# New order of the first Mlp's elementwise steps, with three PSUM banks for its up product and one for its reciprocal

## The chip, the cores and the metric

One core of a Trainium2 chip. The metric is device microseconds of one execution, from start to end on that core. Engines: TensorE (PE) multiplies matrices, VectorE (DVE), ScalarE (ACT) and GpSimd (POOL) do elementwise work, SyncE (SP) issues most transfers. Each engine runs its own instructions in program order and waits on semaphores for the others.

## The reference

A delta-rule attention (4 x 8 heads, 768 steps) gives x of 3072 tokens by 384. Two Mlps follow, each 384 to 2048 to 384. The first, on which the change bears, is

```
h = x @ w_in
P = a0 + a1 h + a2 h^2 + a3 h^3
Q = 1 + |b0| |h| + |b1| h^2
out = (P / (Q + 1e-6)) @ w_out
```

The second has h tanh(softplus(h)) in place of P / Q.

## The kernel before

The attention fills the first 317 us. Then come the Mlps as a loop over **units**: unit i is one of 6 groups of 512 tokens with one of 16 slices of 128 hidden columns, so units 0 to 95 are the first Mlp's and 96 to 191 the second's. Units 0 to 2 are done inside the attention; the loop begins with unit 3. A unit of the first Mlp is nine matmuls up into a PSUM bank `h` (128 x 512; nine, since both operands are split in a high and a low part), a chain of elementwise steps that ends in `gh` (high and low part of g = P / Q), and nine matmuls down that add `gh` times `w_out` into three banks `o`.

`MLP_OPS` writes out the order of one pass of the loop by hand, one string for each Mlp. `u` is the up product, `d` the down product, `y` the evacuation of a finished group's `o` banks (`ev`), `x..` the split of the next group's x into `x_hi` (ScalarE, `xa`) and `x_lo` (VectorE, `xB`), `f c` pieces of the conversion of the second Mlp's weights. `LAGS` says how many passes behind the up product a step runs. The steps of unit i, with the lines of the profile:

- `1a` ScalarE, |h| into q (L929); `1b` b1 q + b0 into r, on GpSimd for odd units and near a group's end (L932), else on ScalarE (L936); `1c` ScalarE, a3 h + a2 into s (L938); `1d` GpSimd, product q r (L942). Lag 0.
- `1e`, `1f` ScalarE, Ln and Exp: the reciprocal, into a PSUM bank `r` (L950, L952). Lag 1.
- `1g`, `1h` VectorE, s times h, then (s + a1) h (L957, L959): the last readers of `h`. Lag 0.
- `1i`, `1j`, `1k` VectorE, one Newton step and P times the reciprocal, with `r` as operand (L966, L970, L975). Lag 1.
- `1L` ScalarE and `1m` GpSimd, the high and the low part of `gh` (L909, L913). Lag 2. The down product has lag 4.

The conversion's VectorE pieces are L749 with L753, L759 and L765; its ScalarE pieces L744 and L772, its GpSimd piece L777. `Ring` hands out tiles of a tag in turn; a tile waits until the last reader of the tile that had its place is done. The eight PSUM banks are two `h`, four `o`, two `r`.

Of the kernel before, what the change touches and what calls it, by code (L numbers as in the profile page):

```python
# [33 lines left out]


MLP_OPS = [
    "fx fw y0 y1 1e 1f u0 u1 u2 1a 1b 1c 1i 1j 1k 1d 1g 1h y2 d0 d1 d2 d3 xa 1L 1m xB f c",
    "fx fw y0 1e 1f y1 2a 2b u0 u1 u2 1i 1j 1k y2 d0 v0 2M d1 v1 d2 v2 d3 v3 xa 1L 1m xB f c",
]
LAGS = {  # L40
# [6 lines left out]
class Ring:  # L47
# [6 lines left out]
    def add(self, pool, **bufs):  # L54
        for tag, b in bufs.items():
            slots = self.slots.setdefault(tag, [])
            self.n[tag] = len(slots)
            slots.extend((pool, b) for _ in range(b))

    def tile(self, shape, dtype, tag):  # L60
        i = self.n[tag]
        self.n[tag] = (i + 1) % len(self.slots[tag])
        pool, b = self.slots[tag][i]
        return pool.tile(shape, dtype, tag=tag, name=tag, bufs=b)


# [174 lines left out]
class Attention:  # L241
# [68 lines left out]
    def load(self, tile, src, u, two=False):  # L310
        o = tile.rearrange("p (n c) d -> p c n d", c=2)
        for a in range(2):
            for c in range(2):
                (self.nc.scalar if two and a else self.nc.sync).dma_start(
                    out=o[64 * a:64 * a + 64, c, :, 0:self.D], in_=src[a][a ^ c][C * u:C * u + C]
                )

    def load_v(self, tile, u):
        o = tile.rearrange("p (c n) d -> p c n d", c=2)
        for a in range(2):  # L320
            for c in range(2):
                self.nc.sync.dma_start(out=o[64 * a:64 * a + 64, c], in_=self.vv[a][c][C * u:C * u + C])
# [594 lines left out]
class Mlp1(Mlp):  # L917
    pool = ()
# [96 lines left out]
class Mlp2(Mlp):  # L1015


    pool = ()
# [32 lines left out]
def tile_delta_attention_two_mlps(  # L1051
# [29 lines left out]
    ps = Ring()  # L1081
# [9 lines left out]
    n1 = len(units)  # L1091
# [6 lines left out]
    def run(fns):  # L1098
        for fn in fns:
            fn()  # L1100
# [6 lines left out]
    def mlp(i):  # L1107
        return m1 if i < n1 else m2

    def starts(i):  # L1110
        return i == 0 or i == n1 or units[i][0] != units[i - 1][0]

    def down(i):

        g, f = units[i]
        m = mlp(i)
        last = i + 1 == n2 or starts(i + 1)

        def out_(d):
            def fn():  # L1120
                acc = m.acc[g][d]
                ev = sb.tile([128, TOK], F32, "ev")
                if i >= n1:
                    nc.scalar.copy(out=ev[:, 0:DM], in_=acc[:, 0:DM])
                    r0 = d * S + g * GU * C
                    nc.sync.dma_start(out=out[r0:r0 + GU * C, :], in_=ev[:, 0:DM])
                    return
                nc.scalar.copy(out=ev, in_=acc)  # L1128
                nc.sync.dma_start(out=x2[g][d * 128:(d + 1) * 128], in_=ev)
            return fn  # L1130

        fns = m.down(i, g, f, starts(i), last)
        return fns, [out_(d) for d in range(len(fns) // 3)] if last else []

    with ExitStack() as actx:
# [35 lines left out]
        for i in range(FIRST):  # L1171
# [6 lines left out]
            else:  # L1178
                r = at.kq[i - 2].rearrange("p s n t -> p (s n t)").rearrange("p (j a t) -> p j a t", j=2, a=2)
# [10 lines left out]
    with ExitStack() as bctx:  # L1190
        sb2 = bctx.enter_context(tc.tile_pool(name="sb2", bufs=1, reuse_waits="tile"))
        ps2 = bctx.enter_context(tc.tile_pool(name="ps2", bufs=1, space=PSUM, reuse_waits="tile"))
        sb.add(sb2, w=NF - FQ - FG, wt=1, w64=1, wm=1, x=1, q=3, s=3, r=2, g=3, gh=5 - FIRST, ev=3)
        ps.add(ps2, h=2, o=4, r=2)
        own = FQ + FG
        fetch_w = {n: (w1.fetch_split, own + LOOK + n) for n in range(NF - own - LOOK)}
        for f in range(DIRECT):
            fetch_w[n1 - NF + 6 + f] = (w2.fetch_split, f)
        calm = [i for i in range(CONV_START, n1 - 8) if not any(starts(i + 5 - k) for k in range(3))]
        for f in range(LOOK):  # L1200
            w1.fetch_split(own + f)
        steps = [
            (m1, "1a", m1.e1, [0]), (m1, "1b", m1.e1, [1]), (m1, "1c", m1.e1, [2]), (m1, "1d", m1.e2, None),
            (m1, "1e", m1.e3, [0]), (m1, "1f", m1.e3, [1]), (m1, "1g", m1.e4, [0]), (m1, "1h", m1.e4, [1]),
            (m1, "1i", m1.e5, [0]), (m1, "1j", m1.e5, [1]), (m1, "1k", m1.e5, [2]),
            (m1, "1l", m1.hi, "V"), (m1, "1L", m1.hi, "A"), (m1, "1P", m1.hi, "P"),
            (m1, "1m", m1.lo, "P"), (m1, "1M", m1.lo, "V"),
            (m2, "2a", m2.e1, None), (m2, "2b", m2.e2, None), (m2, "2M", m2.lo, None),
        ]
        steps = {name: (m, f, a) for m, name, f, a in steps}  # L1210
        ups, downs = {}, {}
        m1.pool = {i for i in range(n1) if i % 2 or any(starts(j) for j in range(i + 3, i + 6) if j < n2)}
        m2.pool = range(n1, n1 + NF)
        for i in range(n2 + max(LG.values())):
            kind = int(i >= n1)
            if i == CONV_START - 3:
                conv.start()

            def at_x(f):
                for k in range(3):  # L1220
                    j = i + 5 - k
                    if 0 < j < n2 and starts(j):
                        f(mlp(j))(units[j][0], k)

            for op in LISTS[kind]:
                if op in steps:
                    m, f, a = steps[op]
                    j = i - LG[op[0] + {"L": "l", "P": "l", "M": "m"}.get(op[1], op[1])]
                    if FIRST <= j < n2 and mlp(j) is m:
                        f(j, *([a] if a else []))  # L1230
                elif op[0] == "u" and FIRST <= i < n2:
                    if i not in ups:
                        ups[i] = mlp(i).up(i, *units[i])
                    n = int(op[1])
                    run(ups[i][3 * n:3 * n + 3])
                elif op[0] == "d" and 0 <= i - FIRST < FIRST:
                    if i - FIRST not in downs:
                        downs[i - FIRST] = down(i - FIRST)
                    n = int(op[1])
                    run(downs[i - FIRST][0][3 * n:3 * n + 3])  # L1240
                elif op[0] in "dvy" and FIRST <= i - LAG - (op[0] == "y") < n2:
                    j = i - LAG - (op[0] == "y")
                    if j not in downs:
                        downs[j] = down(j)
                    n = int(op[1])
                    if op[0] == "d":
                        run(downs[j][0][3 * n:3 * n + 3])
                    elif (op[0] == "y") == (j < n1):
                        run(downs[j][1][n:n + 1])
                elif op == "fw" and i in fetch_w:  # L1250
                    fetch, f = fetch_w[i]
                    fetch(f)
                elif op == "fx" and i + 8 < n2 and starts(i + 8):
                    mlp(i + 8).fetch_x(units[i + 8][0])
                elif op == "xa":
                    at_x(lambda m: m.x_hi)
                elif op == "xB":
                    at_x(lambda m: lambda g, k: m.x_lo(g, k, "V"))
                elif op == "c" and i > n1:
                    w2.free = True  # L1260
                    w2.word = w2.word or ps.tile([128, TOK], F32, "r")[:, 0:384]
                    conv.pull(CONV_RATE)
                elif op == "c" and i in calm:
                    conv.pull(6 * DIRECT * (calm.index(i) + 1) // len(calm) - conv.n)
                elif op == "f":
                    conv.flush()
# [29 lines left out]
```

## Time and profile before

| | us |
|---|---|
| median of 3 runs (lowest, highest) | 1118.54 (1116.56, 1120.43) |
| the profiled execution | 1121.15 |
| its span in the profile | 1119.4 |
| PE busy | 1074.0 (96%) |
| DVE busy | 721.4 (64%) |
| ACT busy | 611.1 (55%) |
| POOL busy | 543.5 (49%) |
| granted TensorE clock, mean | 0.983 |

The shares are means over three stages: the attention (to 317 us), the first Mlp (to about 720 us) and the second. What the change is worth is read from the first Mlp's stretch alone. A row of the timeline is start, duration, engine, line, operation, output <- inputs and the count that is merged into it.

### The profile page before, as it was taken

To read this page: it belongs to the slowest core of one execution; us is meant where nothing else is said; L and a number is where in the kernel's file an instruction comes from. 1 tells how busy PE (TensorE), PEld (TensorE's weight loads), DVE (VectorE), ACT (ScalarE), POOL (GpSimd) and SP (SyncE) were. 2 spreads that over 40 slices of the span, in tenths; PEclk is the share of its full clock that TensorE was granted. 3 is DMA by queue.
4 is the path that set the end of the run, shared out by engine and by line. 5 is a ranking of instruction groups with operands and counts; after the bars stand their busy time and mean duration, and the time that the engine had idled before them with its cause. 6 is when DMAs were issued, how large, how long until landed. Compare 5 with 4: busy or idle time off the path is not lost.

```text
span 1119.4 us, 25084 instructions
## 1 busy us (share of the span) xinstructions
PE 1074.0 (96%) x10396; PEld 935.2 (84%) x10396; DVE 721.4 (64%) x1207; ACT 611.1 (55%) x1099; POOL 543.5 (49%) x626
## 2 busy tenths in 40 slices
PE   8888899898999999999999999999999999999998
PEld 7778888788877788788887888899999999999997
DVE  5895777985779999999999999992121212112110
ACT  4434545243668888889888888643333323323322
POOL 3286987738657777777777777762000000000000
PEclk9898998999999999999999999999999999999999
DMA  9427687324464120212203046240101001010000
GB/s 130 88 50 209 185 218 212 72 60 117 102 242 154 54 72 34 84 41 74 83 15 113 4 139 240 86 155 1 57 1 57 1 22 36 1 57 1 29 1 29
DMA packets 119889, 92.94 MB, mean 83 GB/s; under 512 B 79456, under 2 KB 104160, under 8 KB 119776
## 3 DMA queue, kind: packets, MB, share of 16 engines
q1 hardware_dynamic: 117344, 90.85, 27.9%
q8 instruction: 81, 1.33, 0.5%
q10 hardware_dynamic: 2112, 0.39, 0.2%
q0 software_dynamic: 320, 0.10, 0.1%
q14 instruction: 32, 0.26, 0.1%
HBM read 63.02 MB, written 28.31 MB: 82 GB/s over the span
## 4 chain that ended last, share of the span: by engine, by line
PE 56%; POOL 15%; ACT 8%; DVE 8%; DMA 6%; issue 5%; SPq 1%; POOLq 0%; ACTq 0%; DVEq 0%
PE h L898 23%; PE o L1040 18%; PE o L1007 6%; POOL q L942 5%; DMA kn<-in_k_dram 3%; POOL gh L913 2%; DMA w<-in_moe_w_in_dram 2%; POOL r L932 2%; ACT r L950 2%; PE c_ps L602 2%; PE y_ps L640 2%; POOL xs L531 1%; POOL tmp L525 1%; ACT r L952 1%; ACT q L929 1%
## 5 line engine op out<-in xcount | busy, mean ns | idle before, releaser
L898 PE MATMUL h<-x,w 128*128 128x512 f32 x1278 | 318.0, 393 | 2.8 <-DVE s L959 2.7
L898 PEld LDWEIGHTS h<-x,w 128*128 128x128 f32 x1278 | 236.8, 188 | 55.7 <-DVE s L959 9.2
L913 DVE TENSOR_TENSOR gh<-g,gh 128x512 fp32r<-128x512 f32 x80 | 55.4, 693 | 282.7 <-ACT g L1031 282.7
L1026 ACT ACTIVATE gh<-h 128x512 fp32r<-128x512 f32 x96 | 57.7, 601 | 230.5 <-PE h L898 230.5
L1040 PE MATMUL o<-w,gh 128*128 128x384 f32 x864 | 162.4, 336 | 0.0
L1007 PE MATMUL o<-gh,w 128*128 128x512 f32 x648 | 159.1, 389 | 0.0
L1040 PEld LDWEIGHTS o<-w,gh 128*128 128x128 f32 x864 | 153.4, 188 | 6.0
L913 POOL TENSOR_TENSOR gh<-g,gh 128x512 fp32r<-128x512 f32 x109 | 141.3, 1297 | 23.9 <-ACT g L1031 21.4
L942 POOL TENSOR_TENSOR q<-q,r 128x512 f32<-128x512 f32 x93 | 120.7, 1298 | 60.2 <-ACT r L936 55.8
L1007 PEld LDWEIGHTS o<-gh,w 128*128 128x128 f32 x648 | 121.5, 188 | 26.0 <-ACT ev L1128 0.8
L898 PE MATMUL h<-x,wg 128*128 128x512 f32 x423 | 105.0, 392 | 1.2 <-DVE s L959 1.2
L898 PEld LDWEIGHTS h<-x,wg 128*128 128x128 f32 x423 | 78.7, 188 | 18.0 <-DVE s L959 2.5
L950 ACT ACTIVATE r<-q,cst 128x512 f32<-128x512 f32 x93 | 64.3, 692 | 47.8 <-POOL q L942 47.7
L966 DVE SCALAR_TENSOR_TENSOR q<-q,r 128x512 f32<-128x512 f32 x93 | 63.2, 679 | 14.0 <-ACT r L952 13.7
L938 ACT ACTIVATE s<-h,ab 128x512 f32<-128x512 f32 x93 | 72.0, 774 | 0.0
L959 DVE SCALAR_TENSOR_TENSOR s<-s,ab,h 128x512 f32<-128x512 f32 x93 | 69.6, 748 | 3.3
L970 DVE SCALAR_TENSOR_TENSOR r<-s,ab,r 128x512 f32<-128x512 f32 x93 | 69.4, 746 | 0.0
L531 POOL TENSOR_TENSOR xs<-xs,tmp 128x30 f32<-128x30 f32 (+14 forms) x120 | 63.8, 532 | 9.4
L957 DVE TENSOR_TENSOR s<-s,h 128x512 f32<-128x512 f32 x93 | 63.3, 681 | 4.2 <-ACT s L938 4.2
L975 DVE SCALAR_TENSOR_TENSOR g<-q,r 128x512 f32<-128x512 f32 x93 | 63.9, 687 | 3.2
L525 POOL TENSOR_TENSOR tmp<-xs 128x30 f32<-128x30 f32 (+14 forms) x120 | 58.5, 487 | 7.1
L932 POOL TENSOR_SCALAR r<-q,ab 128x512 f32<-128x512 f32 x53 | 41.4, 782 | 35.3 <-ACT q L929 35.3
(183 smaller groups left out, 1755.2 us busy)
## 6 DMA issues: line engine op xcount, KB each, us to landing
w<-w SPq DMA_DIRECT2D x24, 768.0 KB, 6.7
w<-in_moe_w_in_dram SPq DMA_DIRECT2D x32, 384.0 KB, 3.8
w<-in_moe_w_out_dram SPq DMA_DIRECT2D x32, 384.0 KB, 3.7
xraw<-x SPq DMA_DIRECT2D x36, 256.0 KB, 4.1
w<-wt SPq DMA_DIRECT2D x8, 768.0 KB, 3.3
gh<-in_q_dram SPq DMA_DIRECT2D x48, 96.0 KB, 3.4
v<-in_v_dram SPq DMA_DIRECT2D x48, 96.0 KB, 3.6
x<-yst SPq DMA_DIRECT2D x24, 192.0 KB, 3.4
```

Of the source, the lines that this page charges most:

```text
L525: eng.tensor_tensor(out=tv, in0=ls[:, j, j + 1:HC].unsqueeze(1).to_broadcast([128, j, n]), in1=xs[:, 0:j, j:j + 1].to_broadcast([128, j, n ...
L531: eng.tensor_tensor(out=xs[:, 0:j, j + 1:HC], in0=xs[:, 0:j, j + 1:HC], in1=tv, op=ALU.add)
L898: self.nc.tensor.matmul(out=self.st[i]["h"], lhsT=self.w.t[f][:, a, 0, k], rhs=self.x[g][:, b, k], start=(n == 0), stop=(n == 8),)
L913: (nc.gpsimd if engine == "P" else nc.vector).tensor_tensor(out=s["gh"][:, 1], in0=s["g"], in1=s["gh"][:, 0].bitcast(F32), op=ALU.subtract)
L938: nc.scalar.activation(out=s["s"], in_=s["h"], func=ACTF.Identity, scale=k["a3"], bias=k["a2"])
L942: nc.gpsimd.tensor_tensor(out=s["q"], in0=s["q"], in1=s["r"], op=ALU.mult)
L950: nc.scalar.activation(out=s["r"], in_=s["q"], func=ACTF.Ln, bias=k["c"])
L959: nc.vector.scalar_tensor_tensor(out=s["s"], in0=s["s"], scalar=k["a1"], in1=s["h"], op0=ALU.add, op1=ALU.mult)
L970: nc.vector.scalar_tensor_tensor(out=s["r"], in0=s["s"], scalar=k["a0"], in1=s["r"], op0=ALU.add, op1=ALU.mult)
L975: nc.vector.scalar_tensor_tensor(out=s["g"], in0=s["q"], scalar=2.0, in1=s["r"], op0=ALU.subtract, op1=ALU.mult, reverse0=True)
L1007: self.nc.tensor.matmul(out=self.acc[g][d], lhsT=self.w.t[f][:, a, 1, d], rhs=self.st[i]["gh"][:, b], start=(first and n == 0), stop=(last ...
L1040: self.nc.tensor.matmul(out=self.acc[g][t][:, 0:384], lhsT=self.st[i]["gh"][:, a, t * 128:(t + 1) * 128], rhs=self.w.t[f][:, b, 1].rearran ...
```

## The change

The first string of `MLP_OPS` gets another order: `1e 1f` move from ahead of the up product to behind `1h`, `1i 1j 1k` from ahead of `1d 1g 1h` to behind them, and `1c` goes ahead of `1b`. `Ring.lend` lets a tag take a place from another: one bank, with a tag of its own `hr`, goes to `h` in the first Mlp, and to `r` when the second begins. So the first Mlp has three banks `h`, one `r`, four `o`; the second has what it had.

```
-    "fx fw y0 y1 1e 1f u0 u1 u2 1a 1b 1c 1i 1j 1k 1d 1g 1h y2 d0 d1 d2 d3 xa 1L 1m xB f c",
+    "fx fw y0 y1 u0 u1 u2 1a 1c 1b 1d 1g 1h 1e 1f 1i 1j 1k y2 d0 d1 d2 d3 xa 1L 1m xB f c",
...
-            slots.extend((pool, b) for _ in range(b))
+            slots.extend((pool, b, tag) for _ in range(b))
+
+    def lend(self, pool, tag, to, back=None):
+        if back:
+            self.slots[back].pop()
+            self.n[back] %= len(self.slots[back])
+        self.n[to] = len(self.slots[to])
+        self.slots[to].append((pool, 1, tag))
...
-        pool, b = self.slots[tag][i]
+        pool, b, tag = self.slots[tag][i]
...
-        ps.add(ps2, h=2, o=4, r=2)
+        ps.add(ps2, h=2, o=4, r=1)
+        ps.lend(ps2, "hr", "h")
...
+            if i == n1:
+                ps.lend(ps2, "hr", "r", "h")
```

The lines of the changed kernel stand 7 higher from `Ring` on (L957 becomes L964) and 8 to 10 higher in the loop.

On VectorE, in the first group behind the attention, where one conversion piece and one `x_lo` fall (tile numbers name the allocation: `h_5320`, `h_5361` are the banks of two neighbouring units). Before:

```order
L957 TENSOR_TENSOR s_5332<-s_5332,h_5320 128x512
L959 SCALAR_TENSOR_TENSOR s_5332<-s_5332,ab_77,h_5320 128x512
L765 SCALAR_TENSOR_TENSOR wm_5230<-w64_5049,wm_5230 128x384
L966 SCALAR_TENSOR_TENSOR q_5330<-q_5330,r_5358 128x512
L970 SCALAR_TENSOR_TENSOR r_5358<-s_5332,ab_77,r_5358 128x512
L975 SCALAR_TENSOR_TENSOR g_5379<-q_5330,r_5358 128x512
L957 TENSOR_TENSOR s_5373<-s_5373,h_5361 128x512
L959 SCALAR_TENSOR_TENSOR s_5373<-s_5373,ab_77,h_5361 128x512
L882 TENSOR_TENSOR x_5393<-xraw_5234,x_5393 128x512
```

The same two passes of the changed kernel, where these two units have the banks `h_5317` and `h_5358`:

```order
L973 SCALAR_TENSOR_TENSOR q_5289<-q_5289,r_5336 128x512
L977 SCALAR_TENSOR_TENSOR r_5336<-s_5291,ab_77,r_5336 128x512
L982 SCALAR_TENSOR_TENSOR g_5341<-q_5289,r_5336 128x512
L772 SCALAR_TENSOR_TENSOR wm_5230<-w64_5049,wm_5230 128x384
L964 TENSOR_TENSOR s_5370<-s_5370,h_5358 128x512
L966 SCALAR_TENSOR_TENSOR s_5370<-s_5370,ab_77,h_5358 128x512
L973 SCALAR_TENSOR_TENSOR q_5327<-q_5327,r_5377 128x512
L977 SCALAR_TENSOR_TENSOR r_5377<-s_5329,ab_77,r_5377 128x512
L982 SCALAR_TENSOR_TENSOR g_5382<-q_5327,r_5377 128x512
L889 TENSOR_TENSOR x_5393<-xraw_5234,x_5393 128x512
```

The two steps on a new `h` (L957, L959; now L964, L966) stand ahead of the three steps on the reciprocal of the unit before, and the conversion piece and `x_lo`, which stood behind `1h`, now stand behind `1k`.

On ScalarE at the same place, before:

```order
L950 ACTIVATE r_5317<-q_5292,cst_78 128x512
L952 ACTIVATE r_5317<-r_5317 128x512
L929 ACTIVATE q_5330<-h_5320 128x512
L936 ACTIVATE r_5331<-q_5330,ab_77 128x512
L938 ACTIVATE s_5332<-h_5320,ab_77 128x512
L909 CAST gh_5352<-g_5300 128x512
```

and in the changed kernel:

```order
L936 ACTIVATE q_5327<-h_5317 128x512
L945 ACTIVATE s_5329<-h_5317,ab_77 128x512
L943 ACTIVATE r_5328<-q_5327,ab_77 128x512
L957 ACTIVATE r_5336<-q_5289,cst_78 128x512
L959 ACTIVATE r_5336<-r_5336 128x512
L916 CAST gh_5352<-g_5303 128x512
```

The steps on the new `h` now come ahead of Ln and Exp of the unit before, and `1c` ahead of `1b`. The orders of TensorE, GpSimd and SP are the same in both but for the names of the tiles.

Counted over the 89 passes from the fifth on in that listing, VectorE has no conversion piece and no `x_lo` between `1k` and the next `1g` in 23; in 18 it has an `x_lo`, in 16 each L749 with L753, L759 and L765. Of the 48 conversion places 25 follow a pass with `1b` on ScalarE (9 the pair, 8 L759, 8 L765) and 23 a pass with `1b` on GpSimd (7, 8, 8); all 18 `x_lo` follow the latter. Behind a pass that has none of these stand 8 of the 25, 9 of the 23 and 3 of the 18; behind a pass that has the pair stand 4, 5 and 2.

## Rows read from the trace of the kernel before

**Rows 1.** Windows: length, busy us (count) of PE, PEld, DVE, ACT, POOL, clock, DMA.

```profile
345.00:720.00 375.00, 371.63 (x1617) 300.87 (x1616) 357.85 (x534) 322.48 (x549) 286.69 (x247) 1.00 0.21 75
```

**Rows 2.** Timeline of TensorE, four groups of the first Mlp.

```profile
344.64 2.33 PE L898 MATMUL h<-x,w 128*128 128x512 f32 x9 [0.62 <-DVE s L959]
...
590.24 2.20 PE L1007 MATMUL o<-gh,w 128*128 128x512 f32 x9
592.28 2.20 PE L898 MATMUL h<-x,wg 128*128 128x512 f32 x9
...
712.73 2.20 PE L898 MATMUL h<-x,wg 128*128 128x512 f32 x9
```

**Rows 3.** Line 898's and VectorE's waits, 345 to 720 us: us in total, times.

```profile
  DVE s L959: 14.6, 32
...
DVE q L966 <- ACT r L952: 9.9, 17, 1.0
```

**Rows 4.** VectorE's extras by line and form, 345 to 720 us.

```profile
L882 DVE TENSOR_TENSOR x<-xraw,x 128x512 fp32r<-128x512 f32 x18 | 16.3, 906 | 0.0
L765 DVE SCALAR_TENSOR_TENSOR wm<-w,wm 128x384 int32<-128x384 int32 x16 | 15.0, 938 | 0.0
L759 DVE SCALAR_TENSOR_TENSOR wm<-w,wm 128x384 int32<-128x384 int32 x16 | 12.2, 760 | 0.0
L753 DVE TENSOR_SCALAR wm<-wm 128x384 int32<-128x384 int32 x15 | 11.0, 732 | 0.5
L749 DVE TENSOR_SCALAR wm<-wm 128x384 f32<-128x384 f32 x15 | 9.9, 658 | 0.0
```

**Rows 5.** Timeline of VectorE over one unit with an extra.

```profile
544.45 0.68 DVE L957 TENSOR_TENSOR s<-s,h 128x512 f32<-128x512 f32 x1
545.17 0.75 DVE L959 SCALAR_TENSOR_TENSOR s<-s,ab,h 128x512 f32<-128x512 f32 x1
545.83 0.78 DVE L765 SCALAR_TENSOR_TENSOR wm<-w,wm 128x384 int32<-128x384 int32 x1
546.54 0.68 DVE L966 SCALAR_TENSOR_TENSOR q<-q,r 128x512 f32<-128x512 f32 x1
547.13 0.74 DVE L970 SCALAR_TENSOR_TENSOR r<-s,ab,r 128x512 f32<-128x512 f32 x1
547.91 0.69 DVE L975 SCALAR_TENSOR_TENSOR g<-q,r 128x512 f32<-128x512 f32 x1
548.52 0.68 DVE L957 TENSOR_TENSOR s<-s,h 128x512 f32<-128x512 f32 x1
```

**Rows 6.** Timeline of ScalarE with its neighbours on GpSimd and VectorE, one unit.

```profile
474.30 0.69 ACT L950 ACTIVATE r<-q,cst 128x512 f32<-128x512 f32 x1 [1.08 <-POOL q L942]
...
475.03 0.58 ACT L952 ACTIVATE r<-r 128x512 f32<-128x512 f32 x1
475.52 0.59 ACT L929 ACTIVATE q<-h 128x512 f32<-128x512 f32 x1
475.53 0.55 DVE L759 SCALAR_TENSOR_TENSOR wm<-w,wm 128x384 int32<-128x384 int32 x1
...
476.15 0.82 ACT L936 ACTIVATE r<-q,ab 128x512 f32<-128x512 f32 x1
...
476.87 0.77 ACT L938 ACTIVATE s<-h,ab 128x512 f32<-128x512 f32 x1
477.04 1.30 POOL L942 TENSOR_TENSOR q<-q,r 128x512 f32<-128x512 f32 x1 [1.53 <-ACT r L936]
...
477.53 0.61 ACT L909 CAST gh<-g 128x512 fp32r<-128x512 f32 x1
```

**Rows 7.** GpSimd's linear step `1b` by line, 345 to 720 us.

```profile
L932 POOL TENSOR_SCALAR r<-q,ab 128x512 f32<-128x512 f32 x50 | 39.1, 782 | 30.5 <-ACT q L929 30.5
```

**Rows 8.** Timeline of GpSimd and VectorE at one `x_lo`.

```profile
361.07 1.29 POOL L913 TENSOR_TENSOR gh<-g,gh 128x512 fp32r<-128x512 f32 x1
...
361.38 1.52 DVE L882 TENSOR_TENSOR x<-xraw,x 128x512 fp32r<-128x512 f32 x1
```

## Prediction

> **What bounds the kernel now.** I read the busy table by stretches first, because the whole-page shares mix stages. In the stretch of the first Mlp (345 to 720 us) the clock is granted in full, TensorE is busy 99% and VectorE 95% [rows 1]: two engines that are both almost full. The second Mlp (from 720 us) keeps TensorE busy without a gap and the change touches only its first `r` tile, so its time is taken as it is.
>
> Next the timeline of TensorE. A group of nine matmuls follows the one before in 2.04 us [rows 2], so a unit (nine up, nine down) costs 4.08 us where nothing waits. From unit 10's first matmul at 344.64 to unit 98's at 712.73 [rows 2] lie 88 units: 368.09 us against 88 x 4.08 = 359.0. TensorE loses 9.1 us here. The view of line 898 says to whom: each wait is for step `1h` on VectorE (L959), 32 times [rows 3]. With two `h` banks, unit i+2 can't start before VectorE has done `1h` of unit i, and in the old order `1h` stands behind `1i 1j 1k` of unit i-1 and behind ScalarE's `1e 1f`.
>
> Then VectorE itself. The gaps between starts [rows 5] are 0.72 (`1g` to `1h`), 0.66 (`1h` to the next), 0.59 (`1i` to `1j`), 0.78 (`1j` to `1k`) and 0.61 (`1k` to the next): 3.36 us a unit. On top come what I call extras: one of the three `x_lo` (L882) or a piece of the weight conversion (the pair L749 and L753, or L759, or L765). By the order listing, the 89 cycles from unit 4 on hold 18 `x_lo` and 16 of each piece. With the means of [rows 4], less 0.07 because the next starts that much before an end [rows 5]: 16 x (1.39 + 0.76 + 0.94 - 0.21) + 18 x (0.906 - 0.07) = 61.1 us. VectorE therefore needs 89 x 3.36 + 61.1 = 360.1 us where TensorE needs 89 x 4.08 = 363.1. They are within 1%, so any microsecond added to VectorE soon is one added to the kernel.
>
> **The change, part by part.** *Third `h` bank, and `1g 1h` ahead of `1i 1j 1k`.* An `h` is now free as soon as ScalarE has done `1a 1c` and VectorE `1g 1h`; unit i+3 waits for it, not unit i+2. That takes away the place at which all 32 waits stand. If VectorE's work stays what it is, the most that comes back is the 9.1 us.
>
> *One bank for the reciprocal.* `1e` of unit i (Ln, into the bank) now waits for `1k` of unit i-1. Count from the start of `1k`: it runs 0.69 [rows 5], the handover is put at 0.07 as from ScalarE's L936 to GpSimd's L942 [rows 6], so `1e` starts at 0.76; `1f` 0.73 later at 1.49 and 0.58 long [rows 6], so `1i` can start at 2.14. Without the bank VectorE would be there at 0.61 + 0.72 + 0.66 = 1.99. Idle 0.15 in a cycle with no extra (23 of 89), hidden under the extra in the 66 others, since each of these takes 0.48 or more. Sum 3.5 us. In the old order VectorE's idle time of 9.9 us stands at the same step [rows 3], from the chain over GpSimd; in the new order GpSimd's product (`1d`) has a whole cycle more, so that chain no longer decides. Behind the waiting `1e` on ScalarE stand `1f`, `1L` and the next `1a`, all with a cycle to spare.
>
> *`1c` before `1b`* lets `1g` start earlier; ScalarE runs the same instructions. A cycle of it with `1b` is 0.73 + 0.49 + 0.52 + 0.49 + 0.66 + 0.72 = 3.61 us (spacings of [rows 6], those of `1L` and `1a` put at their length less 0.09), under 4.08. Nothing, but for the five cycles that also hold two evacuations; I leave these to the range. *The bank's return* at the second Mlp restores the old layout: nothing. SP's and GpSimd's orders are unchanged, no transfer moves: nothing.
>
> *Where the extras land* is the part that decides. In the old order they stand behind `1h`, in the new one behind `1k` (the order rows above). How long an extra takes depends on GpSimd: `x_lo` at 361.38 lasted 1.52 us, to 0.54 after the end of the GpSimd subtraction that began at 361.07 [rows 8], while L759 with no GpSimd instruction beside it took 0.55 [rows 6]. I read that as: the extra waits until GpSimd's instruction ends, then runs about 0.54 (`x_lo`) or 0.54 x 384/512 = 0.41 (pieces, an estimate). Both rows show the subtraction only. I take it that the product `1d` holds an extra just as long, since it has the same operands and the same 1.30 us [rows 6]; if it held none, the sum would end at rival 1. The Trainium skill ("SBUF — State Buffer", SBUF: two separate sides) says that VectorE and GpSimd share one pair of ports under an exclusive lock for a whole instruction. By that rule the product holds an extra too, and the sum stays as worked out here; the trace before has no extra beside a product to show it.
>
> Now GpSimd in the new order, from `1k` at 0: `1f` 1.49, `1L` 1.98 to 2.59, subtraction `1m` 2.66 to 3.95; `1a` 2.50, `1c` 2.99. Where ScalarE does `1b`: 3.66 to 4.48, product `1d` 4.55 to 5.85. Where GpSimd does it (0.78 [rows 7]): 3.95 to 4.73, product 4.80 to 6.10; with an `x_hi` on ScalarE all that 0.5 later. The next cycle's extra asks 0.61 after its `1k`, so after an average cycle of 4.05 at 4.66.
> - Behind a ScalarE `1b` (9 pairs, 8 L759, 8 L765): the product has just begun, wait 1.19, then 0.41. L759 1.60 for 0.76, L765 1.60 for 0.94, the pair about 1.9 for 1.39: 9 x 0.5 + 8 x 0.84 + 8 x 0.66 = +16.5 us.
> - Behind a GpSimd `1b` (7 pairs, 8 L759, 8 L765, 18 `x_lo`): single pieces slip in ahead of the product at 0.55, 8 x -0.21 + 8 x -0.39 = -4.8; a pair's second half meets the product, 7 x 0.46 = +3.2; `x_lo` waits 0.59 for the late `1b`, 1.13 for 0.91, 18 x 0.22 = +4.0. Together +2.4.
> - Cycles aren't all average. After one without extra (3.51) the ask comes at 4.12, after one with a pair at about 5.4. By the listing 8 and 4 of the first kind, 9 and 5 pieces and 3 and 2 `x_lo` of the second stand there: -8.4 - 3.0 + 4.1 + 2.8 - 0.8 + 1.2 = -4.1.
>
> Extras +14.8 us. VectorE in the new order: 360.1 + 3.5 + 14.8 = 378.4 over the same 89 cycles. That is more than TensorE's 363.1, so VectorE sets the pace and TensorE loses 15.3 instead of 9.2 (9.1 x 89/88): **+6.1 us**. The extra buffer can't help against an engine that needs more in the mean; it only moves TensorE's wait to the next thing that is late, the `gh` halves that GpSimd's `1m` and ScalarE's `1L` hand to the down product, and the evacuations at a group's end.
>
> **Bounds.** Below: no extra is held at all. Then a piece takes 0.55 and `x_lo` 0.73 at most (0.55 x 512/384): 64 x 0.48 + 18 x 0.66 = 42.6, VectorE 299.0 + 42.6 + 3.5 = 345, TensorE is the limit and all 9.2 come back. Above: the term of 14.8 half as large again, and 4 us for the five cycles with evacuations: 6.1 + 7.4 + 4 = +17.5.
>
> **Rivals.**
> 1. *Faster: the buffer does what it promises.* If extras cost what they cost now, VectorE needs 360.1 + 3.5 = 363.6 against 363.1: about 8.5 us come back, and with a little jitter 6. For it: 32 waits with one releaser [rows 3], and a mean need of VectorE just at TensorE's. Against it: an extra beside a product is what the new order makes common. It decides where the extras' sum grows by less than about 2.5 us. Time 1118.5 - 6 = 1112.5. The Trainium skill ("Perfetto Trace Analysis", Identifying Performance Opportunities) reads gaps that repeat on the engine that should be full as a sign of too few buffers; by that the whole 9.2 would return, 1109.3.
> 2. *No change.* GpSimd itself is held up by VectorE's extras and slides out of the way, so the term is half of mine: VectorE 371, TensorE loses 7.9, -1.3 us. Time about 1117 to 1120.
> 3. *Slower, by the single reciprocal bank or by ScalarE.* Cycles with `1b` on ScalarE and two evacuations are 3.61 + 2 x 0.5 (a copy is about 0.6 long by L909's 0.61 [rows 6], less 0.09) = 4.6, with a conversion step 5.1; five of them, about 4 us, if nothing hides it: on top of mine, 1129.
>
> **How the numbers follow.** The profiled execution took 1121.15 us (span 1119.4); the sum gives 1127.2 for it. The median of the runs is 1118.54, 2.6 lower, so the same difference gives 1124.6, rounded 1125. Chances: my forecast with rival 3, 0.58; rival 2, 0.19; rival 1, 0.23. Faster or slower means by over 0.3% (3.4 us), about what a measurement of this kernel can tell. The range reaches down to rival 1 and up to +14.5 of the bound of +17.5: 1112 to 1133, with some 0.12 below and 0.08 above; the forecast's own range is 1121 to 1133.
>
> **What would show it.** Right: in the stretch of the first Mlp TensorE no longer waits in line 905 (the up product) for `1h`, but in line 1014 for `gh` or `ev`, and for more time in all than 9 us; L766, L772 and the pair's second half (L760) are longer in the mean than now, some near 1.6 us with a product of GpSimd beside them; VectorE's idle time stays small. Wrong: the means of the extras stay as in [rows 4] or fall, then rival 1 or 2 holds; or VectorE idles several microseconds more before `1i`, then the bank alone costs more than the 3.5 us.

## The result, and the profile after

The changed kernel takes 1127.87 us (median of 16 executions, 1120.21 to 1132.44); the kernel before, on the same chip, 1121.46 us (16 executions, 1116.56 to 1128.32). The ratio is 1.0055, 95% interval 1.0038 to 1.0073. That is slower by more than the 0.3% that the prediction took as its bound. A second set of runs of the changed kernel (below) gave 1.0035, 1.0003 to 1.0067. The profiled execution took 1126.96 us, against 1121.15 us for the one of before.

From the page of the changed kernel, the span and the busy time by engine:

```profile
span 1125.2 us, 25174 instructions
## 1 busy us (share of the span) xinstructions
PE 1073.0 (95%) x10396; PEld 940.1 (84%) x10396; DVE 728.8 (65%) x1207; ACT 607.2 (54%) x1099; POOL 553.6 (49%) x626
```

TensorE does the same work as before, VectorE is busy 7.4 us longer and GpSimd 10.1 us longer, though neither has more instructions (1207 and 626, as before). The same window of the first Mlp as in [rows 1] (length, busy us of PE, PEld, DVE, ACT, POOL, clock, DMA):

```profile
345.00:720.00 375.00, 364.39 (x1588) 299.71 (x1587) 361.50 (x529) 318.21 (x545) 292.29 (x245) 0.99 0.21 74
```

TensorE lost 7.2 us of busy time in it and fell from 1617 to 1588 matmuls; VectorE is busier with fewer instructions. The waits in that window (us in total, times, longest), to be held against [rows 3]:

```profile
ACT r L957 <- DVE g L982: 41.7, 49, 2.4
...
PEld o L1014 <- ACT ev L1135: 12.7, 5, 3.3
PE o L1014 <- ACT ev L1135: 10.6, 5, 2.9
...
DVE q L973 <- ACT r L959: 2.4, 6, 0.5
```

TensorE no longer waits for `1h`. It waits five times, once at each group's end, for an evacuation on ScalarE. `1e` on ScalarE (L957) now waits 49 times for VectorE's `1k` (L982), the last reader of the one reciprocal bank. The timeline of TensorE, at unit 10, around one such wait, and at unit 98:

```profile
344.01 2.20 PE L905 MATMUL h<-x,w 128*128 128x512 f32 x9
...
590.09 2.20 PE L905 MATMUL h<-x,wg 128*128 128x512 f32 x9
592.13 0.84 PE L1014 MATMUL o<-gh,w 128*128 128x512 f32 x3
595.88 1.66 PE L1014 MATMUL o<-gh,w 128*128 128x512 f32 x6 [2.91 <-ACT ev L1135]
597.38 2.21 PE L905 MATMUL hr<-x,wg 128*128 128x512 f32 x9
...
718.42 2.20 PE L905 MATMUL h<-x,wg 128*128 128x512 f32 x9
```

Between a group's ends TensorE runs without a gap. At a group's end the evacuation that frees an `o` bank is late: three matmuls go into the bank that is free, the other six wait, and the next up product starts 3.2 us later than a full rate would have it (597.38 less 590.09 is 7.29, against 4.08). From unit 10 to unit 98 lie 374.41 us: TensorE loses 15.4 of them, where before it lost 9.1. Not all of this is waiting: behind two of the five waits the granted clock falls to 1.2 GHz, the lower of its two levels, for some 3 us (mean 0.79 from 388 to 396 us, 0.57 from 526 to 530), and the nine up matmuls from 527.77 on take 3.12 us instead of 2.04. From unit 10 to 98 the clock is 0.991 in the mean, about 3.4 us of TensorE's time; before it was 1.000.

VectorE's extras by line and form, the counterpart of [rows 4] (L760 was L753, L766 was L759, L889 was L882, L772 was L765, L756 was L749):

```profile
L760 DVE TENSOR_SCALAR wm<-wm 128x384 int32<-128x384 int32 x15 | 18.2, 1210 | 0.5
L766 DVE SCALAR_TENSOR_TENSOR wm<-w,wm 128x384 int32<-128x384 int32 x16 | 14.1, 883 | 0.0
L889 DVE TENSOR_TENSOR x<-xraw,x 128x512 fp32r<-128x512 f32 x18 | 14.0, 780 | 0.0
L772 DVE SCALAR_TENSOR_TENSOR wm<-w,wm 128x384 int32<-128x384 int32 x16 | 13.1, 822 | 0.0
L756 DVE TENSOR_SCALAR wm<-wm 128x384 f32<-128x384 f32 x15 | 10.8, 720 | 0.0
```

The pair's second half went from 732 to 1210 ns and L766 from 760 to 883; `x_lo` and L772 became shorter. Why is seen in the timeline of GpSimd and VectorE, four places:

```profile
361.80 1.29 POOL L939 TENSOR_SCALAR r<-q,ab 128x512 f32<-128x512 f32 x1
...
361.82 0.71 DVE L889 TENSOR_TENSOR x<-xraw,x 128x512 fp32r<-128x512 f32 x1
...
460.51 1.29 POOL L949 TENSOR_TENSOR q<-q,r 128x512 f32<-128x512 f32 x1 [2.00 <-ACT r L943]
...
460.56 1.66 DVE L766 SCALAR_TENSOR_TENSOR wm<-w,wm 128x384 int32<-128x384 int32 x1
...
526.79 0.55 DVE L766 SCALAR_TENSOR_TENSOR wm<-w,wm 128x384 int32<-128x384 int32 x1
...
541.11 1.29 POOL L949 TENSOR_TENSOR q<-q,r 128x512 f32<-128x512 f32 x1
541.27 1.34 DVE L760 TENSOR_SCALAR wm<-wm 128x384 int32<-128x384 int32 x1
```

A piece of 0.55 us (526.79, nothing of GpSimd beside it) takes 1.66 us when it asks just after a product has begun (460.56), and the pair's second half 1.34 (541.27). The other way round, at 361.8, `x_lo` gets 0.71 and GpSimd's `1b` beside it 1.29 instead of the 0.78 of [rows 7]. Whichever is held, one of the two pays.

**A ledger of VectorE.** The experiments are compared by one account, made from the timeline of VectorE between unit 10 and unit 98. Each distance from one start to the next is booked: behind `1g 1h 1i 1j 1k` the spacing of [rows 5] as base (0.716, 0.663, 0.599, 0.782, 0.605 in the mean) and what is above it as idle; behind an extra the whole distance. A wait that follows an extra is therefore booked with the extra: 7.0 us of them in e6, 1.4 to 1.6 in the two traces of the changed kernel and in e10, at most 0.5 in the others. The window also holds 83 extras in the kernel before, in e3, e6 and e10, 84 in e2, 85 in e7b and 86 in the others; three more are about 2 us. Beside it stands the stage, from the first up product of the loop (unit 3) to unit 98, and the ratio of times.

| kernel | unit 10 to 98 | base | extras | idle | stage | ratio, 95% interval |
|---|---|---|---|---|---|---|
| before | 368.1 | 294.7 | 61.2 | 11.8 | 395.6 | 1 |
| changed | 374.4 | 295.3 | 70.2 | 8.4 | 401.9 | 1.0055 (1.0038 to 1.0073) |
| changed, again | 372.8 | 296.7 | 65.8 | 10.1 | 399.5 | 1.0035 (1.0003 to 1.0067) |
| e1: order alone | 365.3 | 296.1 | 67.7 | 1.2 | 392.0 | 0.9971 (0.9942 to 1.0001) |
| e2: banks alone | 371.0 | 295.4 | 62.5 | 12.9 | 397.7 | 1.001 (0.9981 to 1.004) |
| e4: order, two `h`, one `r` | 371.2 | 295.3 | 68.8 | 6.5 | 397.9 | 1.007 (1.0034 to 1.0107) |
| e12: e4 again | 371.7 | 296.1 | 69.1 | 6.5 | 398.3 | 0.9996 (0.9961 to 1.003) |
| e3: e4, words of the pieces in PSUM | 360.7 | 295.3 | 47.6 | 17.2 | 387.4 | 0.9926 (0.9897 to 0.9955) |
| e6: e3 in the old order | 367.4 | 294.7 | 55.5 | 16.9 | 395.8 | 0.9978 (0.995 to 1.0006) |
| e5: changed, evacuations early | 370.1 | 296.1 | 64.1 | 9.6 | 396.8 | 1.0014 (0.9985 to 1.0043) |
| e10: e3, evacuations early | 360.2 | 296.1 | 48.3 | 15.6 | 386.9 | 0.9924 (0.9886 to 0.9962) |
| e11: e1, evacuations early | 365.1 | 296.1 | 68.3 | 0.7 | 391.8 | 0.9956 (0.9929 to 0.9982) |
| e7: changed, pieces behind `1h` | 369.5 | 297.4 | 61.3 | 11.2 | 396.4 | 1.0029 (0.9998 to 1.0061) |
| e7b: e1, pieces behind `1h` | 377.8 | 296.7 | 74.9 | 5.4 | 406.2 | 1.007 (1.0041 to 1.0098) |

TensorE's own 88 units are 359.0. The stage of the kernels run twice came out 2.4 us apart (changed) and 0.4 us apart (e4); the ratio of the latter moved from 1.007 (7 executions) to 0.9996 (12), more than each interval allows. The attention ahead of the stage differs from one execution to the next (unit 3 begins at 309 to 325 us), while what follows unit 98 takes 406.6 to 406.8 us in all fourteen traces. So below a per cent the stage of a trace is the better witness, and no cause is read from less than 2.5 us of it. The kernel before has one trace only.

### The profile page after: what moved, and what is told of

The parts are those of the page before. It is cut to its first block, busy times and chain, and to the rows that moved or that the text cites. A ratio compares the mean times of both kernels' runs of the same rounds, so it can differ in the third digit from the quotient of the medians.

```text
span 1125.2 us, 25174 instructions
## 1 busy us (share of the span) xinstructions
PE 1073.0 (95%) x10396; PEld 940.1 (84%) x10396; DVE 728.8 (65%) x1207; ACT 607.2 (54%) x1099; POOL 553.6 (49%) x626
## 4 chain that ended last, share of the span: by engine, by line
PE 50%; DVE 24%; ACT 9%; DMA 7%; issue 5%; POOL 3%; SPq 2%; ACTq 0%; DVEq 0%; POOLq 0%
PE h L905 19%; PE o L1047 18%; DVE q L973 4%; DVE r L977 4%; DVE g L982 4%; PE o L1014 3%; DMA w<-in_moe_w_in_dram 2%; PE y_ps L647 2%; DMA kn<-in_k_dram 2%; ACT r L957 2%; DVE s L964 2%; PE c_ps L609 2%; ACT r L959 2%; DMA w<-w 2%; SPq L321 1%
## 5 line engine op out<-in xcount | busy, mean ns | idle before, releaser
L905 PE MATMUL h<-x,w 128*128 128x512 f32 x1071 | 264.9, 391 | 0.0
L905 PEld LDWEIGHTS h<-x,w 128*128 128x128 f32 x1071 | 200.0, 188 | 38.5
L1014 PE MATMUL o<-gh,w 128*128 128x512 f32 x648 | 161.6, 393 | 10.6 <-ACT ev L1135 10.6
L1014 PEld LDWEIGHTS o<-gh,w 128*128 128x128 f32 x648 | 121.9, 189 | 38.0 <-ACT ev L1135 12.7
L949 POOL TENSOR_TENSOR q<-q,r 128x512 f32<-128x512 f32 x93 | 124.3, 1337 | 37.4 <-ACT r L943 21.7
L957 ACT ACTIVATE r<-q,cst 128x512 f32<-128x512 f32 x92 | 63.8, 694 | 45.0 <-DVE g L982 42.3
L905 PE MATMUL h<-x,wg 128*128 128x512 f32 x351 | 87.8, 395 | 0.0
L905 PEld LDWEIGHTS h<-x,wg 128*128 128x128 f32 x351 | 66.5, 190 | 13.1
L982 DVE SCALAR_TENSOR_TENSOR g<-q,r 128x512 f32<-128x512 f32 x92 | 63.2, 687 | 3.2
L916 ACT CAST gh<-g 128x512 fp32r<-128x512 f32 x93 | 57.2, 615 | 0.4 <-DVE g L982 0.4
L1038 ACT ACTIVATE g<-h 128x512 f32<-128x512 f32 x96 | 57.1, 595 | 0.0
L959 ACT ACTIVATE r<-r 128x512 f32<-128x512 f32 x92 | 53.5, 582 | 2.9
L1047 PE MATMUL o<-wg,gh 128*128 128x384 f32 x288 | 54.4, 337 | 0.0
```

The costliest lines, as they stand in the source:

```text
L905: self.nc.tensor.matmul(out=self.st[i]["h"], lhsT=self.w.t[f][:, a, 0, k], rhs=self.x[g][:, b, k], start=(n == 0), stop=(n == 8),)
L949: nc.gpsimd.tensor_tensor(out=s["q"], in0=s["q"], in1=s["r"], op=ALU.mult)
L957: nc.scalar.activation(out=s["r"], in_=s["q"], func=ACTF.Ln, bias=k["c"])
L959: nc.scalar.activation(out=s["r"], in_=s["r"], func=ACTF.Exp, scale=-1.0)
L982: nc.vector.scalar_tensor_tensor(out=s["g"], in0=s["q"], scalar=2.0, in1=s["r"], op0=ALU.subtract, op1=ALU.mult, reverse0=True)
L1014: self.nc.tensor.matmul(out=self.acc[g][d], lhsT=self.w.t[f][:, a, 1, d], rhs=self.st[i]["gh"][:, b], start=(first and n == 0), stop=(last ...
```

## The experiments

The diffs are against the changed kernel. First the change was taken apart.

**e1, the new order with the old banks** (two `h`, two `r`):

```
-        ps.add(ps2, h=2, o=4, r=1)
-        ps.lend(ps2, "hr", "h")
+        ps.add(ps2, h=2, o=4, r=2)
...
-            if i == n1:
-                ps.lend(ps2, "hr", "r", "h")
```

> New order of the steps, banks as before (two h, two r). Theory A (VectorE sets the pace, and its conversion pieces are held by GpSimd's product in the new order): the pieces last as long as in the changed kernel, 4 to 8 us slower than before; TensorE's waits go back to the up product. Rival B (the single reciprocal bank costs it): with two banks 0 to 3 us faster than before. Rival C (TensorE's waits for the evacuations cost it): with two banks TensorE can't run ahead, so no such waits and within 3 us of before.

Measured 1117.69 us, 0.9971, with an interval that just reaches 1; the stage is 3.6 us shorter than before, and 3.8 in e11, which has this order and these banks too. That is rival B's forecast and not theory A's, though the extras did grow: VectorE has almost no idle time left (1.2 us), its extras take 6.5 us more (about 2 of it for three more of them in the window), and TensorE waits for `1h` again, but less (waits of e1, first Mlp):

```profile
PEld h L905 <- DVE s L966: 7.2, 10, 1.5
PE h L905 <- DVE s L966: 3.7, 6, 1.0
...
DVE q L973 <- ACT r L959: 1.5, 3, 0.5
```

So by the stage the order alone is a gain: it takes away 10.6 us of VectorE's idle time, nearly all of it ahead of `1i`, and gives 6.5 back in extras.

**e2, the new banks with the old order:** the changed kernel with the first string of `MLP_OPS` as it was before.

> Old order, banks as in the change (three h, one r). Theory A: the pieces stand behind 1h and last as before; the third h bank gives a little back, 0 to 5 us faster than before, unless the single r bank binds. Rival B: 5 us slower or more, with VectorE idle before 1i. Rival C: TensorE runs ahead and waits for the evacuations, 4 to 8 us slower.

Measured 1121.33 us, 1.001; stage +2.1 us, within what two traces of one kernel differ. The waits of e2:

```profile
DVE q L973 <- ACT r L959: 10.1, 18, 1.0
...
PE o L1014 <- ACT ev L1135: 8.2, 5, 2.2
...
PEld h L905 <- DVE s L966: 1.8, 1, 1.8
```

The third `h` bank does take away the wait for `1h` (32 times before, once here), and TensorE then waits as long at the five evacuations. VectorE's wait for the reciprocal is what it was. Rival C named the waits, but no kernel 4 to 8 us slower came of them, and theory A's gain didn't come either.

**e4 and e12, the new order with two `h` and one `r`,** the eighth bank left empty:

```
-        ps.lend(ps2, "hr", "h")
...
-                ps.lend(ps2, "hr", "r", "h")
+                ps.lend(ps2, "hr", "r")
```

> New order, two h, one r, the eighth bank left empty in the first Mlp: the control of the run before. Theory A: as the changed kernel or up to 4 us slower than it (6 to 10 slower than before). Rival B: as the changed kernel. Rival C: within 3 us of before, as TensorE can't run ahead.

> The new order with two h banks and one for the reciprocal (the eighth bank empty), once more: the one trace of it was taken of the fastest of its executions, and its medians stood 11.7 us above those of the same order with two reciprocal banks, where the traces show only 5.9 us. Theory (the single bank costs 6 to 10 us, in idle time before 1i and in extras that meet GpSimd's product; a third h bank gives nothing back): the stage at 398 to 402 us, idle 6 to 10, extras 66 to 70, ratio 1.003 to 1.008, not to be told from the changed kernel's 1.0055. Rival (the third h bank gives or costs something by itself): the stage and the ratio more than 0.3% from the changed kernel's, to one side.

Measured 1129.41 us, 1.007, and then 1121.21 us, 0.9996. The second ratio lies below the forecast of 1.003 to 1.008. The two traces agree to half a microsecond, so they are used: stage 397.9 and 398.3, as forecast. Against e1 (392.0), which differs by the second reciprocal bank alone, the single bank costs 5.9 to 6.3 us, nearly all of it as idle time of VectorE (6.5 against 1.2). The changed kernel, which has a third `h` bank on top, is 1.2 to 4.0 us slower than these two by the traces; none shows a gain from that bank, and a cost of it is not settled. One candidate is the clock, 0.991 from unit 10 to 98 in both traces of the changed kernel and 1.000 in e4 and e12, where TensorE's longest wait for an evacuation is 1.4 us instead of 2.9; no run tests it.

**e8, the changed kernel once more,** nothing edited:

> The changed kernel once more, nothing edited: it gives the spread by which one trace may differ from another of the same kernel. If the split of VectorE's time read so far (extras 70.2, idle 8.4, 374.4 us for 88 units) is a property of the order, all three come out within 1.5 us, five waits for an evacuation included, and the stage (unit 3 to 98) within 1.5 of 401.9. If the phase of GpSimd wanders from one execution to the next, extras or idle differ by several microseconds, and readings of single terms under that size are not to be made. The ratio to before 1.003 to 1.008 either way.

Measured 1124.85 us, 1.0035. The terms moved by more than 1.5 us: extras 65.8 instead of 70.2, idle 10.1 instead of 8.4. Nearly the whole difference of the extras (4.1 of 4.4) is the pair's second half, by the lines of VectorE in e8:

```profile
L760 DVE TENSOR_SCALAR wm<-wm 128x384 int32<-128x384 int32 x15 | 14.1, 942 | 0.5
```

942 ns against 1210: the phase between VectorE and GpSimd isn't the same in each execution. So the second alternative came. What does repeat is the place of TensorE's waits (four evacuations, 8.7 us) and, to some 3 us, the sum of extras and idle time.

Then the cost under dispute, the extras that GpSimd holds.

**e3, e4 with the conversion pieces' words in the empty PSUM bank.** The same instructions, with the word that the pieces build up in PSUM instead of SBUF:

```
-        ps.add(ps2, h=2, o=4, r=1)
-        ps.lend(ps2, "hr", "h")
+        ps.add(ps2, h=2, o=4, r=1, word=1)
+        w2.word = ps.tile([128, TOK], F32, "word")[:, 0:384]
```

> New order, two h, one r, and the eighth bank as the place for the conversion pieces' intermediate words (in the second Mlp such pieces took 0.56 us beside GpSimd). Theory A: the four pieces fall to about 0.56 us each, VectorE's extras from about 70 to about 44 us, and the kernel is 5 to 9 us faster than before and at least 10 faster than the same kernel without this place. Rivals B and C: no faster than that kernel, since the bank loop and the evacuations are the same.

Measured 1113.67 us, 0.9926, faster than both kernels. This is theory A's forecast. VectorE's extras by line in e3 (the window takes in the first pieces of the second Mlp, hence more of them):

```profile
L889 DVE TENSOR_TENSOR x<-xraw,x 128x512 fp32r<-128x512 f32 x18 | 16.2, 898 | 0.0
L766 DVE SCALAR_TENSOR_TENSOR word<-w,word 128x384 int32<-128x384 int32 x21 | 11.7, 557 | 0.1
L772 DVE SCALAR_TENSOR_TENSOR wm<-w,word 128x384 int32<-128x384 int32 x21 | 11.5, 548 | 0.1
L760 DVE TENSOR_SCALAR word<-word 128x384 int32<-128x384 int32 x20 | 11.3, 566 | 0.7
L756 DVE TENSOR_SCALAR word<-wm 128x384 f32<-128x384 f32 x20 | 11.1, 554 | 0.1
```

and its timeline at one pair:

```profile
660.53 1.30 POOL L920 TENSOR_TENSOR gh<-g,gh 128x512 fp32r<-128x512 f32 x1
661.08 0.55 DVE L756 TENSOR_SCALAR word<-wm 128x384 f32<-128x384 f32 x1
661.66 0.57 DVE L760 TENSOR_SCALAR word<-word 128x384 int32<-128x384 int32 x1
```

Each piece now takes its 0.55 us, the first of these inside a GpSimd instruction and the second begun in it; only `x_lo`, left as it was, is still long (898). The extras fall from 68.8 to 47.6 us (about 2 of this is three extras fewer in the window), VectorE has 17.2 us to spare, and TensorE is within 1.7 us of its own 359.0. In the first Mlp the one thing changed against e4 is where a piece's word lies, and the stage is 10.5 us shorter: that is what the pieces held by GpSimd cost there. (In the second Mlp e3 has one reciprocal bank less; the time behind unit 98 is 406.8 us in both.)

**e6, the same words in PSUM in the old order:** e3 with the old string.

> Old order, two h, one r, the eighth bank for the conversion pieces' words. Theory A: extras fall from 61 to about 47 us as in the new order with this place, VectorE has time to spare, and the stretch comes to within 3 us of that kernel's 387.4 (4 to 8 us faster than before). If the order matters by itself (its chain of h over GpSimd to Exp holds TensorE in the old one), it stays 4 us or more behind the new order with this place.

Measured 1118.6 us, 0.9978, stage 395.8 against 395.6 before. Its waits:

```profile
DVE q L973 <- ACT r L959: 19.1, 40, 1.2
PEld h L905 <- DVE s L966: 13.1, 33, 1.8
```

The pieces do fall as forecast. With the waits behind an extra counted as idle time, the extras go from 61.0 to 48.5 us and the idle time from 12.0 to 23.9: nearly all that is saved turns into waiting for the reciprocal, and TensorE waits 33 times for `1h` as before (32). So in the old order VectorE's sum does not set the pace, and the second forecast holds (8.4 us behind e3). What does is the chain over the reciprocal, by these waits; in the new order cheaper work on VectorE pays.

Last, two places that the trace of the changed kernel pointed to.

**e5, the evacuations one pass earlier:**

```
-    "fx fw y0 y1 u0 u1 u2 1a 1c 1b 1d 1g 1h 1e 1f 1i 1j 1k y2 d0 d1 d2 d3 xa 1L 1m xB f c",
+    "fx fw u0 u1 u2 1a 1c 1b 1d 1g 1h 1e 1f 1i 1j 1k d0 d1 d2 d3 xa y0 y1 y2 1L 1m xB f c",
...
-                elif op[0] in "dvy" and FIRST <= i - LAG - (op[0] == "y") < n2:
-                    j = i - LAG - (op[0] == "y")
+                elif op[0] in "dvy" and FIRST <= i - LAG - (op[0] == "y" and kind) < n2:
+                    j = i - LAG - (op[0] == "y" and kind)
```

> The changed kernel with a group's three evacuations one pass earlier on ScalarE (behind the down product that they read, ahead of 1L). Theory A (VectorE sets the pace; the wait for the evacuations is only where TensorE's lead ends): TensorE's waits move to the gh halves or the up product, the first Mlp's stretch stays within 2 us of the changed kernel's 401.9. Rival C (the evacuations cost it): the 10.6 us of waits go and 6 to 10 us come back.

Measured 1120.53 us, 1.0014, stage 396.8: 5.1 us below the first trace of the changed kernel, 2.7 below the second. That is neither theory A's forecast (within 2) nor rival C's (6 to 10). Four waits for an evacuation are left (6.8 us), and the extras are lower too (64.1). The same edit was therefore made to two kernels in which TensorE hardly waits for an evacuation, **e10** (on e3) and **e11** (on e1).

> The pieces' words in PSUM (as in the fastest kernel so far) and the evacuations one pass earlier. Theory A (what is left there is TensorE's own time, the evacuations cost 0.8 us in one wait): the stage stays within 1.5 us of 387.4, the ratio within 0.002 of 0.9926. Rival (the evacuations take time from ScalarE and VectorE at each group's end that returns elsewhere): 2 to 4 us less, ratio about 0.990.

> The new order with the old banks (two h, two for the reciprocal) and the evacuations one pass earlier. In the order alone the trace has no wait for an evacuation that counts; VectorE is full (idle 1.2 us) and TensorE waits 7.2 us for h. Theory A (VectorE's sum decides, the waits for evacuations of the changed kernel are where its lateness shows): no gain, the stage within 2 us of 392.0 and the ratio within 0.002 of 0.9971. Rival (the place of the evacuations costs by itself, as the gain of 5 us from the same edit on the changed kernel suggests): 3 to 5 us less, ratio about 0.993.

Measured 1111.89 us, 0.9924, and 1116.52 us, 0.9956; the stages are 0.5 and 0.2 us from those of e3 and e1, as theory A has it in both. The place of the evacuations costs nothing where VectorE has time or two reciprocal banks. What the edit gave on the changed kernel is some 3 to 5 us by the traces, with intervals of the ratio that overlap; how much of that is the evacuation and how much the phase of the extras stays open.

**e7, the pieces behind `1h`,** as in the old order, with the new banks, and **e7b**, the same string with the old banks:

```
+    "fx fw y0 y1 u0 u1 u2 1a 1c 1b 1d 1g 1h c 1e 1f 1i 1j 1k y2 d0 d1 d2 d3 xa 1L 1m xB f",
```

> The changed kernel with the conversion pieces moved from behind 1k to behind 1h; x_lo stays. Theory A: a piece now asks 2.0 us after the start of 1k, when GpSimd's product is at its end and the subtraction has not begun; the pieces fall from 57 to 45 us or less, and fill the wait for the single bank too: 6 to 12 us faster than the changed kernel. If the length of the pieces is not what costs, the time stays within 2 us of the changed kernel. Rival B alone: 2 to 4 us, from the filled wait.

> New order, banks as before (two h, two r), conversion pieces behind 1h. Theory A: there is hardly any idle time left on VectorE to fill (1.2 us in the order alone), so only shorter pieces can help; if they fall by 5 us or more the stretch falls from 392.0 toward TensorE's 386, else no change against the order alone.

Measured 1124.6 us, 1.0029, and 1128.99 us, 1.007. In e7 the extras go back to 61.3 us and the idle time rises to 11.2, and the stage, 396.4, is 5.5 us under the changed kernel's first trace and 3.1 under its second, about where it was before: less than theory A's 6 to 12. In e7b the extras grow to 74.9 instead, which neither forecast had. A wait that e1 hardly has (1.1 us) may be a part of the reason, though no run separates it: ScalarE's conversion step stands in the same pass as the piece that it reads (waits of e7b),

```profile
ACT wt L779 <- DVE wm L772: 26.3, 15, 2.3
```

26.3 us in which ScalarE's own steps queue behind it. So the piece's place in a pass isn't good or bad by itself: it decides what a piece meets, and that depends on the banks too.

The best version found is the new order with one reciprocal bank, two `h` and the freed bank for the pieces' words: e3 and e10, 0.9926 and 0.9924, which their intervals don't tell apart.

## Why the prediction came out as it did

The forecast was 1125.0 us with a range of 1112 to 1133, and slower with a chance of 0.58. It came out at 1127.87. The sum said that VectorE would need 378.4 us in 89 cycles, that is 374.1 in the 88 units from 10 to 98; they took 374.4 and, in the second trace, 372.8. TensorE was to lose 15.3 us and lost 15.4 and 13.8. The total and the place of TensorE's wait were right. But two terms were mis-sized in opposite directions, and one view of the kernel before was wrong: that the total fits so closely is luck.

*The extras.* The mechanism was right: the product holds an extra (1.34 and 1.66 us at 541.27 and 460.56), which no row of before showed. The Trainium skill ("SBUF — State Buffer", SBUF: two separate sides) says that the pair of ports is held for a whole instruction, and the trace agrees: the piece at 541.27 ends 0.21 us after the product. The term was too large. The ledger's extras grew by 9.0 and 4.6 us, of which about 2 is three more extras in the window and 1.3 waits behind an extra. By the means of the lines, for 16 of each piece and 18 `x_lo`, the growth is 6.5 us in the first trace and 1.6 in the second, where 14.8 was predicted. By kind, in the first trace: the pair +8.6 (its second half meets the product; the prediction gave it +7.7 ahead of its corrections for uneven cycles), L766 +2.0, L772 -1.9, `x_lo` -2.3. The term that was mis-sized is the one that set the asks of L766, L772 and `x_lo` against GpSimd's product: between unit 10 and 98 of the first trace a running product was met by 8 of 17 L766, as the sum had it, but by only 3 of 17 L772, where it had 8 too (9 began ahead of a product), and 2 of 18 `x_lo`. The sum let GpSimd run as if nothing held it. It is held as well: its `1b` is 879 ns in the mean instead of 782 and the product 1340 instead of 1298. And its subtraction waits for ScalarE's `1L`, which it hardly did before (first line before, second changed, 345 to 720 us):

```profile
POOL gh L913 <- ACT gh L909: 2.5, 6, 0.7
POOL gh L920 <- ACT gh L916: 46.3, 62, 2.3
```

That is the mechanism of rival 2, and it took away more than half of the term; that these two holds moved the asks is argued from the rows, no run sets them apart.

*The single reciprocal bank.* Predicted 3.5 us of idle time, 0.15 in each of 23 cycles without an extra. In the changed kernel the idle time is 8.4 and 10.1 us. By e1 and e4, whose only difference it is, the bank costs 5.3 us of idle time. In the first trace 17 of the 22 cycles without an extra idle 0.21 or 0.22 instead of 0.15, and all 22 together 5.2 us; 1.6 us more stand ahead of `1i` in cycles with an extra, where the prediction had none, and 1.4 behind `1k`. What the prediction had wrong, or left to its range, is in the timeline of TensorE, ScalarE and VectorE of the changed kernel at a group's end:

```profile
520.84 2.20 PE L905 MATMUL h<-x,wg 128*128 128x512 f32 x9
...
523.38 0.69 ACT L957 ACTIVATE r<-q,cst 128x512 f32<-128x512 f32 x1 [1.78 <-DVE g L982]
...
525.11 1.08 ACT L1135 COPY ev<-o 128x512 f32<-128x512 f32 x2
...
525.75 2.23 PE L1014 MATMUL o<-gh,w 128*128 128x512 f32 x6 [2.03 <-ACT ev L1135]
...
526.06 0.62 ACT L936 ACTIVATE q<-h 128x512 f32<-128x512 f32 x1
526.55 0.80 ACT L945 ACTIVATE s<-h,ab 128x512 f32<-128x512 f32 x1
...
527.21 0.84 ACT L943 ACTIVATE r<-q,ab 128x512 f32<-128x512 f32 x1
...
527.92 0.71 ACT L957 ACTIVATE r<-q,cst 128x512 f32<-128x512 f32 x1
...
528.66 0.58 ACT L959 ACTIVATE r<-r 128x512 f32<-128x512 f32 x1
...
529.36 0.69 DVE L973 SCALAR_TENSOR_TENSOR q<-q,r 128x512 f32<-128x512 f32 x1 [0.50 <-ACT r L959]
```

`1e` at 523.38 has waited 1.78 us for VectorE's `1k`, since there is one bank. The prediction put behind it only `1f`, `1L` and the next `1a`, "all with a cycle to spare", and left the five cycles with two evacuations to its range. At a group's end the evacuations stand there too: they come late, TensorE waits 2.03 us for them, and `1a` begins at 526.06 on an `h` that was complete at 523.04. From there ScalarE has no gap, and `1i` waits 0.50 for a reciprocal whose inputs had long been there. So VectorE's lateness is paid at TensorE and once more on VectorE. The same is seen once more, at 599.49; two other idle times of this length follow an `h` that TensorE delivered late. This is rival 3 in part, the bank together with the ScalarE cycle that holds two evacuations. TensorE's waits for `ev` are the symptom of VectorE's lateness, handed on by the one bank: e4 has five of them (6.5 us), e3, with the same string and reciprocal bank but cheaper extras, one of 0.8 us, and e1, with two banks, none (waits of the matmuls).

*The third `h` bank, rival 1.* It was to bring back up to 9.2 us, or, with a little jitter, 6. In the old order it takes the waits for `1h` away and gives nothing (e2); in the new order e4 and e12 without it are no slower by their stages. The rule of the Trainium skill ("Perfetto Trace Analysis", Identifying Performance Opportunities) that repeated gaps can mean too few buffers pointed at the wrong place here: the gaps were at `h`, and what was late was VectorE (new order) or the chain over the reciprocal (old order).

*The order, and what was misread of the kernel before.* The prediction put VectorE's need of 360.1 within 1% of TensorE's 363.1 and concluded that a microsecond added to VectorE is one added to the kernel. For the old order e6 speaks against it: 12.5 us less of extras moved its 88 units by 0.7. (e6 also has one reciprocal bank less than before; e2, which has a third `h` bank besides, puts that at 1.1 us of idle time.) The idle time of 11.8 us, 9.9 of it in waits before `1i` [rows 3], which the prediction counted as slack, belongs to the chain that set the pace. The pages of the kernel before and of the changed one show it in the chain of work that ended last, by engine, over the whole execution:

```profile
PE 56%; POOL 15%; ACT 8%; DVE 8%; DMA 6%; issue 5%; SPq 1%; POOLq 0%; ACTq 0%; DVEq 0%
PE 50%; DVE 24%; ACT 9%; DMA 7%; issue 5%; POOL 3%; SPq 2%; ACTq 0%; DVEq 0%; POOLq 0%
```

Before, it ran over GpSimd and hardly over VectorE; in the changed kernel it is the other way round. Hence the order alone was not the loss that the prediction's terms make it (360.1 + 14.8 = 374.9 in 89 cycles, 2.6 us more than before in 88 units) but a gain of 2.8 us, and the single bank, at 5.9 to 6.3 us of the stage, took more than that back. The total came out right since the term of the extras was too high (by 8.3 and 13.2 us) by more or less what the idle time was too low (8.4 and 10.1 in the ledger, 9.8 and 11.7 with the waits behind an extra, where 3.5 were predicted).

What the prediction said would be seen was seen in the line and releaser of TensorE's wait (L1014 for `ev`, 10.6 us), and in L760 and L766. L772 fell where it was to rise, as did `x_lo` where the sum had it rise. VectorE's idle time is less than before, but two to three times the 3.5 us of the sum: the sign that the bank alone costs more.

## What to carry to other kernels

When an engine is almost full, ask of a reordering which work it puts next to which: here the same instructions cost VectorE 47.6 to 74.9 us by what ran on GpSimd beside them and by where their words lay. A wait that always names one buffer isn't yet a reason for another buffer: find what is late behind it, and what the bank was doing where it is taken from. And put a term that depends on the phase of two engines down with a range as wide as itself; two traces of one kernel gave 6.5 and 1.6 us for it.

## What was not expected of the hardware

- A VectorE instruction on 128 x 384 with its word, as input or output, in PSUM and at most one input in SBUF is not held by GpSimd: 548 to 566 ns in the mean in e3, inside GpSimd instructions of 1.30 us, against 720 to 1210 ns with the word in SBUF in the changed kernel. The pair's two steps pay for it where nothing holds them: 0.35 and 0.36 us at the shortest with the word in SBUF, 0.55 and 0.57 everywhere in e3.
- The hold works both ways: GpSimd's `1b` of 0.78 us took 1.29 beside an `x_lo` that began 0.02 us after it (361.80).
- Two executions of the same program can settle into different phases of two engines: the same line took 942 and 1210 ns in the mean, with the times of the two stages 2.4 us apart.
